# A pooled-attention and mixing kernel on one core: the 1e-9 of the softmax sums as a 73rd column, the pools' 1/8 moved to the copies of x, a subtraction in two pieces, and a new order

## The chip, the core and the metric

The kernel runs on one of the eight cores of a Trainium2 chip. A core has five engines, each with its own queue of instructions that it works off in order: TensorE (PE, with its weight loads shown as PEld), VectorE (DVE), ScalarE (ACT), GpSimd (POOL) and SyncE (SP), which here only issues DMAs. They wait for each other through semaphores. The metric is the device time of one execution in microseconds; the median of three runs is compared.

## The reference, cut to what matters

```python
k_p = k.reshape(B, H, Sp, 8, D).mean(axis=3)        # B, H, S, D = 8, 8, 576, 64; Sp = 72
v_p = v.reshape(B, H, Sp, 8, D).mean(axis=3)
scores = q @ k_p.T / sqrt(D)
attn = exp(scores - scores.max(-1))
attn = attn / (attn.sum(-1) + 1e-09)
x = (attn @ v_p) as [8, 576, 512]
theta = x @ w_theta
y = w_tok_r @ (x * cos(theta)) + w_tok_i @ (x * sin(theta))
u = x + y
out = u + maximum(u @ w_ch, 0)
```

q, k and v come as float32, the four weights as float64, which the kernel turns into float32 itself. The pooled keys and values are kept as sums over 8 rows, not as means, so a factor 1/8 has to be applied to each somewhere: for the keys it is in the scale of the exponential, for the values it is what the change moves.

## The kernel before, in words

All products that need float32 accuracy are made of two rounded parts, a high and a low one (`xh`, `xl` of `x`; `zh`, `zl` of `z`; `uh`, `ul` of `u`; `th`, `tl` and so on of the weights), and three matmuls: high by high, high by low, low by high. The high part is a rounding copy on any engine, the low part a subtraction on DVE or POOL.

The program is a set of generators, one for each step of each batch, and a `yield` ends each piece of a step. A table of words, `SCHEDULE`, names which generator runs its next piece, and a letter behind the word (`a`, `v`, `g`) gives the engine for a piece that can run on several (ACT, DVE, POOL). So the table is the whole order of the program: each engine gets its instructions in the order in which the words stand. Nothing in it is decided while the kernel runs. The words are:

- `k`, `v`, `Q`, `w`, `h`, `c`: loads of keys, values, queries and weights, and their conversion; `K`, `V`: pooling and placing of keys and values; `D`: 24 idle matmul instructions (12 matmuls on an identity tile, line 256)
- `Sb.m` (`soften`): one tile `m` of the attention of batch `b`: scores on PE (lines 661 and 669) into one PSUM tile, maximum (700), subtraction (716), exponential on ACT (720), row sums of 8 heads (722), `sm = (sm + 1e-9) * 8` (729), reciprocal (731), the products `en = e / sm` (734 and 741), and from batch 2 on a transpose of 32x32 blocks into one shared tile `G` (750, 753). Tiles 0 and 1 make the first group of a batch, tiles 2, 3 and 4 the second. In batches 0 and 1 the sums come with the exponentials of ACT, head by head (709), and in batch 0 the 1e-9 and the 8 are put in by ACT (726).
- `Eb.g` (`turn`): 16 DMAs that finish the transpose of a whole group from `G` to `eraw` (816), and its split in two parts (819 to 839). `G` has one buffer, so the next group's write to it has to wait for these DMAs.
- `Xb.g.c` (`attend`): attention times values (863), and a copy of the result from PSUM to `xT` (865; the helper is at lines 175 and 177)
- `Tb.m` (`rotate`): theta (886), cosine and sine, and `z` (913 to 923)
- `Zb.c` (`take`): `zh` and `zl` of 128 of the 512 columns of `z` (935 and 937); `Mb.c.h` (`mix`): the 27 matmuls of the token mix for one such block and one part of the rows (951), the addition to `xT` (957), `uh` and `ul` (962, 964). Part `h=0` has 256 rows and uses `zl` in its last nine matmuls, part `h=1` has 320 rows and uses `zl` in its first nine. Two PSUM buffers serve `py` and the `pf` of the next step.
- `Fb.c.h` (`final`): the last product (980), its addition (986), a transpose (999) and the store (1005).

While one batch is in `M`, the next but one is in `S` and `E`; while it is in `F`, the next one is in `T`.

Of the kernel before, what the change touches and what calls it, by code (L numbers as in the profile page):

```python
# [35 lines left out]
w0.1a S0.3 S0.1v X0.0.0 w2.0 S0.2g S0.2g S0.2 X0.0.0a h1v h1 h3 h3 h3v S0.2a S0.2 S0.4 S0.4 S0.4 h2 w0.1 h3v
w0.1 h3 h3 h3v S0.3g S0.3g S0.3 S0.2a X0.0.1 X0.0.1v h3 h3a X0.0.3 X0.0.3a S0.3a S0.4 w0.1g W0 S0.4g S0.4g k1.1
w1.1 w1.1 w1.1a h2v S0.4 S0.4a S0.4 S0.4a h2 X0.0.2 W0v W0 h3 X0.0.2a T0.0v K1.1g S0.3 S0.3a X0.2.0 w3.1 T0.1v
T0.1g w2.0 w2.0a w2.0v T0.0g X0.2.0a W0 W0v W0 w2.1 w2.1 k1.2 w1.1a w1.1 w1.1 Q1.0 Q1.1 w3.0 Q1.1 Q1.1a Q1.0
Q1.0a X0.2.3 X0.2.3a w2.0 X0.2.1 X0.2.1a w2.1a w2.1a w2.1 w1.1v w2.1 w2.1g T0.0 T0.0 T0.0 v1.0 V1.0g W1 W1v W1  # L40
w3.0 T0.0 T0.0 T0.0a X0.2.2 X0.2.2v T0.2g w3.0a w3.0v K1.2g T0.0 T0.0 Q1.2 Q1.3 Q1.3 Q1.3v T0.1 T0.1 W1 w3.1
w3.1a X0.2.3g T0.0 W1v T0.1 T0.1 T0.1 Q1.2 T0.1a W1 T0.2v T0.2 w2.0 w2.0v w3.0 w3.0 w3.1a w3.1 T0.4a v1.1 T0.2
T0.2 T0.3a T0.3g T0.1 T0.1 T0.1 W2 W2a W2 T0.2 T0.2 c0 T0.2a T0.2 T0.2 T0.2 Q1.2a T0.3 T0.3 w4.0 w4.0 w4.0a
T0.4g T0.4 w3.0g T0.3 T0.3 T0.3 T0.3a w4.0v w4.0 w3.1 V1.1g T0.4 W2 w4.0 W2a W2 T0.4 w3.1v W3 T0.4 T0.4 T0.3
T0.3 T0.3 c0 c0a w4.0g Q1.4 Q1.4 T0.4 T0.4 W3a K1 K1a K1 W3 c0 W4 c0 c0 c0g Z0.0a Z0.0v M0.0.0 c0g c0g W4a W4
W4a W4 W4a W4 W4a W4 c1 M0.0.0 W3 W3a W3 Z0.1v Z0.1v M0.0.1 c1 c1a c1 c1 c1 K1a c1v c1a k2.2 K2.2v c1v c2 Z0.2a
M0.0.0a M0.0.1 M0.0.1a S1.0 S1.0 c2 M0.1.0 M0.1.0 Q1.4v c2v c2 c2 v1.2 V1.2v c2 c2v M0.1.1 M0.1.1 M0.1.1v S1.0
S1.0 S1.0v Z0.3a Z0.3v c2a c2v Z0.2g M0.2.0 M0.2.0 S1.0v V1a V1g V1 c3 M0.1.0v M0.1.0g c3 S1.1 S1.1 S1.1 c3v c3
c3 c3 c3g c3a c3g M0.2.1 M0.1.1g M0.2.1 S1.0 S1.0v S1.0 S1.0 S1.0a M0.3.0 S1.1 S1.1v S1.1v M0.2.0a M0.2.0g S1.0
S1.2 S1.2 S1.2 S1.1 S1.1v S1.1 S1.1 S1.1v S1.1 M0.3.1 V1g M0.3.0 M0.3.0a V1g S1.2 X1.0.0 X1.0.0a M0.3.1 M0.3.1a  # L50
S1.2v S1.2v S1.3 S1.3 S1.3 M0.3.0g X1.0.1 X1.0.1v M0.0.0g M0.0.1v M0.2.1g M0.2.1g M0.3.1v F0.0.0 X1.0.3 F0.0.0
X1.0.3v F0.0.1 F0.0.1 F0.0.0 F0.0.1 X1.0.2 k2.0 S1.2 K2.0g X1.0.2a S1.3 S1.2a S1.2 S1.2 S1.2a S1.4 S1.4 S1.2
Q2.0 Q2.0 S1.3g v2.2 S1.3g F0.1.1 F0.1.1 S1.3 S1.3v S1.3 S1.3 S1.4 S1.4 S1.4v S1.4v T1.0g S1.3a S1.3 T1.0g T1.0
T1.0 T1.0 T1.0 S1.4 S1.4a S1.4 S1.4 S1.4a S1.4 F0.1.0 F0.0.1 X1.2.0 X1.2.0v T1.0 T1.0a T1.0 k2.1 K2.1g K2 K2a
Q2.1 Q2.1 X1.2.3 X1.2.3a T1.1g T1.1g T1.1 T1.0 T1.0 F0.1.0 F0.1.0 X1.2.1 X1.2.1a v2.0 V2.2g V2.0v v2.1 T1.1 T1.1
T1.1 X1.2.2 X1.2.2a T1.3v F0.1.1 F0.1.1 T1.2g T1.2g T1.3g V2.1g V2g k3.2 K2 K2a S2.0 S2.0 T1.1 T1.1a F0.2.0
F0.2.0 T1.1 T1.1 T1.1 S2.0 S2.0 T1.2 T1.2 T1.2 S2.0g S2.0v F0.2.1 T1.2 F0.2.1 F0.2.0 F0.2.1 T1.2 T1.2a X1.2.3a
k3.0 S2.1 S2.1 K3.2g K3.0g T1.2 T1.2 T1.2 S2.0 S2.1 S2.1 S2.1g T1.3 T1.3 S2.1g T1.3 T1.3 S2.1 S2.2 S2.2 T1.4a
T1.4g Q3.0 V2g T1.3 T1.3a T1.3 F0.2.1 V2 V2g V2g T1.3 T1.3 F0.3.0 F0.3.0 F0.3.0 T1.4 T1.4 T1.4 T1.4 T1.4 S2.3
k3.1 S2.2 K3.1v K3 S2.2 S2.2g T1.4 T1.4 S2.2v F0.3.1 F0.3.1 Z1.0a Z1.0v M1.0.0 S2.3 Z1.1a Z1.1g E2.0 S2.2 S2.4  # L60
# [1065 lines left out]
```

## Time and profile before

| what | value |
|---|---|
| median of 3 runs | 633.87 us (633.78 to 636.93) |
| the profiled execution | 635.37 us, of which span 633.6 us |
| PE busy | 602.3 us (95%) |
| DVE busy | 482.1 us (76%) |
| ACT busy | 300.8 us (47%) |
| POOL busy | 354.1 us (56%) |
| instructions | 11412 |
| mean granted TensorE clock | 0.977 |

The share of busy time is an average over stages of different kinds: loads and weight conversion up to about 76 us, the first batch with the rest of the conversion up to about 182 us, then the steady part, then the last product. "Idle before" in a group of instructions is time in which the engine stood still just ahead of them, and the name behind it is what ended the wait. A busy PE is not a PE at its peak, since matmuls are pipelined and their ends are modelled. An engine's idle time costs nothing unless something waits for what it does next.

### The profile page before, as it was taken

To read this page: it belongs to the slowest core of one execution; us is meant where nothing else is said; L and a number is where in the kernel's file an instruction comes from. 1 tells how busy PE (TensorE), PEld (TensorE's weight loads), DVE (VectorE), ACT (ScalarE), POOL (GpSimd) and SP (SyncE) were. 2 spreads that over 40 slices of the span, in tenths; PEclk is the share of its full clock that TensorE was granted. 3 is DMA by queue.
4 is the path that set the end of the run, shared out by engine and by line. 5 is a ranking of instruction groups with operands and counts; after the bars stand their busy time and mean duration, and the time that the engine had idled before them with its cause. 6 is when DMAs were issued, how large, how long until landed. Compare 5 with 4: busy or idle time off the path is not lost.

```text
span 633.6 us, 11412 instructions
## 1 busy us (share of the span) xinstructions
PE 602.3 (95%) x4120; PEld 556.4 (88%) x4120; DVE 482.1 (76%) x893; ACT 300.8 (47%) x655; POOL 354.1 (56%) x382
## 2 busy tenths in 40 slices
PE   7899989799899999999999999899999999999995
PEld 6766879788689989998899989888999999999995
DVE  6587979988878989689876888867977698556233
ACT  5577956567863454237532573036524452144110
POOL 2345631656764667867657677665448545541520
PEclk9599969899999999999999999999999999999999
DMA  9972412345855647473625546235444240511204
GB/s 291 245 229 67 113 43 70 70 84 116 141 95 95 107 93 134 89 125 72 110 53 101 98 87 140 44 56 104 82 69 71 48 66 10 82 19 26 33 2 76
DMA packets 235130, 57.85 MB, mean 91 GB/s; under 512 B 223169, under 2 KB 223681, under 8 KB 235073
## 3 DMA queue, kind: packets, MB, share of 16 engines
q1 hardware_dynamic: 233888, 56.97, 45.6%
q8 instruction: 33, 0.54, 0.4%
q10 hardware_dynamic: 1184, 0.15, 0.2%
q14 instruction: 25, 0.20, 0.1%
HBM read 37.81 MB, written 9.44 MB: 75 GB/s over the span
## 4 chain that ended last, share of the span: by engine, by line
PE 66%; DVE 17%; SPq 6%; ACT 3%; DMA 3%; issue 2%; POOL 0%; DVEq 0%; ACTq 0%; POOLq 0%
PE py L951 24%; PE pf L980 13%; PE pt L886 13%; SPq L816 6%; PE pv L863 6%; PE s L669 3%; PE px L896 2%; DMA eraw<-G 2%; DVE ul L964 1%; DVE mx L700 1%; DMA kpst<-in_k_dram 1%; DVE G L750 1%; PE pq L577 1%; PE s L661 1%; DVE en L734 1%
## 5 line engine op out<-in xcount | busy, mean ns | idle before, releaser
L951 PE MATMUL py<-WTh,zh 128*128 128x256 f32 (+1 forms) x576 | 87.8, 300 | 3.9 <-DVE xT L957 2.7
L951 PE MATMUL py<-WTl,zh 128*128 128x256 f32 (+1 forms) x576 | 88.8, 300 | 0.0
L951 PE MATMUL py<-WTh,zl 128*128 128x256 f32 (+1 forms) x576 | 86.4, 297 | 0.0
L951 PEld LDWEIGHTS py<-WTh,zh 128*128 128x128 f32 x576 | 81.0, 191 | 4.8 <-issue 1.8
L951 PEld LDWEIGHTS py<-WTl,zh 128*128 128x128 f32 x576 | 82.0, 194 | 0.0
L951 PEld LDWEIGHTS py<-WTh,zl 128*128 128x128 f32 x576 | 78.9, 191 | 0.2
L937 POOL TENSOR_TENSOR zl<-z,zh 128x1152 fp32r<-128x1152 f32 x20 | 55.1, 2759 | 31.4 <-ACT zh L175 19.1
L879 POOL TENSOR_TENSOR xl<-xT,xh 128x512 fp32r<-128x512 f32 x33 | 44.6, 1357 | 43.6 <-ACT xh L175 30.8
L957 DVE TENSOR_TENSOR xT<-py,xT 128x256 f32<-128x256 f32 (+1 forms) x64 | 28.1, 442 | 42.9 <-PE py L951 42.9
L964 POOL TENSOR_TENSOR ul<-xT,uh 128x256 fp32r<-128x256 f32 (+1 forms) x40 | 33.8, 857 | 34.0 <-ACT uh L175 18.9
L720 ACT ACTIVATE e<-e 128x576 f32<-128x576 f32 (+1 forms) x30 | 20.6, 686 | 60.0 <-DVE e L716 59.9
L980 PE MATMUL pf<-uh,chh 128*128 128x320 f32 (+1 forms) x256 | 46.7, 305 | 0.0
L980 PE MATMUL pf<-ul,chh 128*128 128x320 f32 (+1 forms) x256 | 45.6, 298 | 0.9 <-DVE ul L964 0.9
L886 PE MATMUL pt<-th,xh 128*128 128x512 f32 x160 | 44.9, 402 | 0.2
L890 ACT ACTIVATE g<-pt,c_magic 128x512 f32<-128x512 f32 x38 | 26.1, 686 | 39.6 <-PE pt L886 32.9
L980 PE MATMUL pf<-uh,chl 128*128 128x320 f32 (+1 forms) x256 | 44.5, 296 | 0.0
L886 PE MATMUL pt<-th,xl 128*128 128x512 f32 x160 | 43.4, 393 | 0.6 <-POOL xl L879 0.6
L886 PE MATMUL pt<-tl,xh 128*128 128x512 f32 x160 | 43.8, 396 | 0.0
L669 PE MATMUL s<-kpT,qT 128*128 128x144 f32 x256 | 40.8, 306 | 2.0 <-DVE ri L731 0.9
L175 ACT COPY xT<-pv 128x320 f32<-128x320 f32 (+1 forms) x43 | 17.1, 398 | 50.2 <-PE pv L863 46.9
L669 PEld LDWEIGHTS s<-kpT,qT 128*128 128x128 f32 x256 | 36.3, 203 | 3.8 <-ACT spare L709 1.2
L980 PEld LDWEIGHTS pf<-ul,chh 128*128 128x128 f32 x256 | 38.0, 189 | 1.7 <-DVE ul L964 1.7
(250 smaller groups left out, 1441.0 us busy)
## 6 DMA issues: line engine op xcount, KB each, us to landing
out_dram<-R SPq DMA_DIRECT2D x112, 72.0 KB, 2.1
kpst<-in_k_dram SPq DMA_DIRECT2D x15, 512.0 KB, 4.1
vpst<-in_v_dram SPq DMA_DIRECT2D x28, 256.0 KB, 3.8
qsst<-in_q_dram SPq DMA_DIRECT2D x96, 72.0 KB, 3.3
eraw<-G SPq DMA_DIRECT2D x96, 60.0 KB, 2.3
eraw<-G SPq DMA_DIRECT2D x96, 40.0 KB, 2.1
WTh_st<-in_moe_w_theta_dram SPq DMA_DIRECT2D x4, 512.0 KB, 8.7
wcraw<-in_moe_w_ch_dram SPq DMA_DIRECT2D x4, 512.0 KB, 3.9
```

The source lines that it names most:

```text
L669: nc.tensor.matmul(scs[c // 2][:n, 2 * SP * (c % 2) : 2 * SP * (c % 2 + 1)], qT[:, c, t0 : t0 + n], kpT[:, c, :], start=True, stop=True,)
L720: nc.scalar.activation(e[:n], e[:n], AF.Exp, scale=scale)
L816: nc.sync.dma_start(blocks(Ex, jj, i), blocks(Gx, i, jj))
L863: nc.tensor.matmul(pv[:, :gn], l, r, start=i == 0, stop=i == len(terms) - 1)
L879: ENG[pick()].tensor_tensor(xl, xT[:, :, o], f32(xh), ALU.subtract)
L886: nc.tensor.matmul(pt, l[:, c, :], r[:, c, :], start=i == 0, stop=i == 11)
L890: nc.scalar.activation(g, pt, AF.Identity, bias=c_magic)
L937: ENG[pick()].tensor_tensor(zl, z[:, :, o], f32(zh), ALU.subtract)
L951: nc.tensor.matmul(py[:, :n], l[:, kk, :], r[:, kk, t], start=i == 0, stop=i == 3 * NK - 1)
L957: nc.vector.tensor_tensor(u, py[:, :n], u, ALU.add)
L964: ENG[pick()].tensor_tensor(ul[:, c, t], u, f32(uh[:, c, t]), ALU.subtract)
L980: nc.tensor.matmul(pv[:, :n], l[:, kk, o], uhl[r][:, kk, t], start=i == 0, stop=i == 11)
```

## The change

Four edits, beside the order. (1) The exponentials go to one constant tile `e_eps` of 8 x 73 columns, of which column 73 holds 1e-9 from a fill at the start; the row sum is taken over all 73, which makes the separate `(sm + 1e-9) * 8` on DVE go. (Tiles 1 and 3 of batch 0 keep their own tile.) In batches 0 and 1, where the sums come from ACT, the 1e-9 is added by an instruction of ACT right behind the exponentials. (2) The 1/8 of the pooled values is applied where `xT` is copied from PSUM: the copy becomes an activation with a scale on ACT, or a multiplication on DVE. (3) `zl` is made by two instructions, of 640 and 512 columns a partition, on the same engine. (4) The zero tile at the start is a part of `G`. The line numbers move by one to three: what was line 722 is 727, 731 is 729, 734 is 732, 750 is 748, 951 to 964 are three higher.

```diff
+    e_eps = const([P, 8, SP + 1], F32, "e_eps")
+    nc.gpsimd.memset(e_eps, 1e-9)
+
+    G = const([P, 5 * 3 * P], F32, "G")
+    nc.gpsimd.memset(G, 0.0)
+    zero = G[:, 0:512]
...
-        e = temp(b, m, "e", 8 * SP).rearrange("p (x g) -> p x g", g=SP)
+        if split:
+            e = temp(b, m, "e", 8 * SP).rearrange("p (x g) -> p x g", g=SP)
+        else:
+            e = e_eps[:, :, 0:SP]
...
                     bias=mx[:n, x : x + 1], scale=scale, accum_out=sm[:n, x : x + 1],
                 )
+            nc.scalar.activation(sm[:n], sm[:n], AF.Identity, bias=c_eps[:n])
             yield
...
             nc.scalar.activation(e[:n], e[:n], AF.Exp, scale=scale)
             yield
-            nc.vector.tensor_reduce(sm[:n], e[:n], AX.X, ALU.add)
-            if b == 0:
-                yield
-        if b == 0:
-            nc.scalar.activation(sm[:n], sm[:n], AF.Identity, bias=c_eps[:n], scale=float(POOL))
-            yield
-        else:
-            nc.vector.tensor_scalar(sm[:n], sm[:n], 1e-9, float(POOL), ALU.add, ALU.mult)
+            nc.vector.tensor_reduce(sm[:n], e_eps[:n], AX.X, ALU.add)
...
-        copy(pick(), xT[:, c, g0 : g0 + gn], pv[:, :gn])
+        if pick() == "a":
+            nc.scalar.activation(xT[:, c, g0 : g0 + gn], pv[:, :gn], AF.Copy, scale=1.0 / POOL)
+        else:
+            nc.vector.tensor_scalar(xT[:, c, g0 : g0 + gn], pv[:, :gn], 1.0 / POOL, None, ALU.mult)
...
-        ENG[pick()].tensor_tensor(zl, z[:, :, o], f32(zh), ALU.subtract)
+        for r in (slice(0, 5), slice(5, NK)):
+            ENG[pick()].tensor_tensor(zl[:, r], z[:, r, o], f32(zh[:, r]), ALU.subtract)
```

The order is a new table from its first word to its last; a line of each, the first one:

```diff
-D k0.2 w0.0 w0.0 w0.0a w0.0v w0.0 h0 h0 h0a k0.0 K0.0 h0a h0 h0 h0v h0 h0v h0 h2 h2 k0.1 K0.1 h2a h2a h1 h2 h2
+k0.0 w0.0 k0.1 K0.0 K0.1 w0.0 w0.0a w0.0g w0.0 h0 h0 h0g h0a h0 h0 h0v h1 k0.2 h1 h1a h1a h1 h1 h1g Q0.0 K0.0a
```

Three places show what the table does. First, the head of PE's queue, up to the first scores `s`. Before:

```order
L256 MATMUL warm<-ident 128x128 x12
L516 MATMUL kpp_136<-kpst_0_134,ident 128x128 x8
L350 MATMUL ths_149<-WTh_st,ident 128x512
L351 MATMUL ths_149<-WTl_st,identr 128x512
L516 MATMUL kpp_136<-early,ident 128x128 x8
L518 MATMUL kpp_136<-kprst_119,ident 64x64 x8
L527 MATMUL pk_187<-ident,kp_182 64x128 x4
L577 MATMUL pq_0_198<-ident,qsst_0_196 128x128 x4
L537 MATMUL pkr_206<-ident,kpr_183 64x64
L669 MATMUL s_0_209<-kpT,qT_195 128x144 x4
```

and in the changed kernel:

```order
L517 MATMUL kpp_111<-kpst_0_106,ident 128x128 x8
L517 MATMUL kpp_111<-early,ident 128x128 x8
L519 MATMUL kpp_111<-kprst_144,ident 64x64 x8
L528 MATMUL pk_169<-ident,kp_155 64x128 x4
L578 MATMUL pq_0_177<-ident,qsst_0_153 128x128 x4
L351 MATMUL ths_183<-WTh_st,ident 128x512
L352 MATMUL ths_183<-WTl_st,identr 128x512
L538 MATMUL pkr_188<-ident,kpr_156 64x64
L670 MATMUL s_0_191<-kpT,qT_152 128x144 x4
L257 MATMUL warm<-ident 128x128 x12
```

The idle matmuls went from the front of PE's queue to behind the first scores. On SP's queue the first block of keys (`kpst`) went with them from fourth to first, and the last block (`kprst`) from first to sixth.

Second, DVE at the last tile of the attention of batch 5 (`sm_4`, `en_4`), which runs during the token mix of batch 4 (`py_1_0`). Before:

```order
L722 TENSOR_REDUCE sm_4_4648<-e_4_4646 64x8
L729 TENSOR_SCALAR sm_4_4648<-sm_4_4648 64x8
L731 RECIPROCAL ri_4_4736<-sm_4_4648 64x8
L734 TENSOR_TENSOR en_4_4738<-e_4_4646,ri_4_4736 64x512
L741 TENSOR_TENSOR en_4_4738<-e_4_4646,ri_4_4736 64x64
L750 STREAM_TRANSPOSE G<-en_4_4738 64x4x128
L753 STREAM_TRANSPOSE G<-en_4_4738 64x64
L554 STREAM_TRANSPOSE qT_4326<-qsst_1_4779 128x1152
L957 TENSOR_TENSOR xT_3776<-py_1_0_4751,xT_3776 128x256
```

and in the changed kernel:

```order
L727 TENSOR_REDUCE sm_4_4690<-e_eps 64x8
L729 RECIPROCAL ri_4_4740<-sm_4_4690 64x8
L732 TENSOR_TENSOR en_4_4742<-e_eps,ri_4_4740 64x512
L739 TENSOR_TENSOR en_4_4742<-e_eps,ri_4_4740 64x64
L748 STREAM_TRANSPOSE G<-en_4_4742 64x4x128
L751 STREAM_TRANSPOSE G<-en_4_4742 64x64
L960 TENSOR_TENSOR xT_3754<-py_1_0_4705,xT_3754 128x256
L177 CAST uh_4733<-xT_3754 128x256
L555 STREAM_TRANSPOSE qT_4221<-qsst_1_4672 128x1152
```

The scalar instruction is gone, and the eviction of `py_1_0` went ahead of the transpose of the queries.

Third, DVE a little later, where the next attention tile (batch 6, tile 0) writes `G` again and the block `py_2_1` is evicted. Before:

```order
L722 TENSOR_REDUCE sm_0_4884<-e_0_4882 128x8
L729 TENSOR_SCALAR sm_0_4884<-sm_0_4884 128x8
L731 RECIPROCAL ri_0_4889<-sm_0_4884 128x8
L734 TENSOR_TENSOR en_0_4891<-e_0_4882,ri_0_4889 128x512
L741 TENSOR_TENSOR en_0_4891<-e_0_4882,ri_0_4889 128x64
L750 STREAM_TRANSPOSE G<-en_0_4891 128x4x128
L753 STREAM_TRANSPOSE G<-en_0_4891 128x64
L177 CAST eh_256_4895<-eraw_256_4894 128x1280
L957 TENSOR_TENSOR xT_3776<-py_2_1_4916,xT_3776 128x320
```

and in the changed kernel:

```order
L727 TENSOR_REDUCE sm_0_4848<-e_eps 128x8
L729 RECIPROCAL ri_0_4852<-sm_0_4848 128x8
L443 TENSOR_TENSOR kprst_4585<-kprst_4585 64x256
L443 TENSOR_TENSOR kprst_4585<-kprst_4585 64x128
L448 TENSOR_TENSOR kpr_4855<-kprst_4585 64x64
L177 CAST eh_256_4891<-eraw_256_4890 128x1280
L1002 STREAM_TRANSPOSE R_3_4910<-oT_3_1_4593 128x320
L960 TENSOR_TENSOR xT_3754<-py_2_1_4862,xT_3754 128x320
L1002 STREAM_TRANSPOSE R_3_4910<-oT_3_0_4564 128x256
L748 STREAM_TRANSPOSE G<-en_0_4914 128x4x128
L751 STREAM_TRANSPOSE G<-en_0_4914 128x64
```

The write to `G` went from ahead of the eviction of `py_2_1` to behind it, and the products `en` of this tile went to POOL.

Over the whole program the table moves 11 of the 40 subtractions `xl` from POOL to DVE (7 there before, 18 now).

More of the change, by code (lines that the diff above doesn't have):

```diff
@@ L36 @@
[L36 to L60, printed above, removed]
@@ new lines @@
+F0.0.0 F0.0.0 F0.0.0 F0.0.1 S1.3 S1.3 X1.0.3 X1.0.3a S1.2 S1.2a S1.2 S1.2 S1.2a S1.4 S1.4 S1.3g S1.3g S1.3
+F0.1.1 S1.2 k2.1 K2.1v Q2.0 T1.0g T1.0v S1.4 S1.4 S1.3a S1.3 S1.3 S1.3a S1.3 F0.0.1 T1.0 T1.0 S1.4g S1.4g S1.4
+T1.0 S1.4a S1.4 S1.4 v2.0 S1.4a S1.4 F0.1.0 F0.1.0 V2.0v T1.0 T1.0 T1.0a T1.1g T1.0 T1.0 T1.0 X1.2.0 X1.2.0a
+F0.1.1 K2 K2v Q2.1 T1.1g T1.1 T1.1 X1.2.3 X1.2.3a T1.1 T1.1 X1.2.2 X1.2.2a T1.1 K2 K2a X1.2.1 T1.1a X1.2.1a
+T1.2a v2.1 V2.1g V2g V2g Q2.1 S2.0 S2.0 k3.2 T1.3a k3.0 T1.2v T1.2 T1.1 T1.1 T1.3g T1.1 S2.0 T1.2 F0.1.0 F0.1.1
@@ new lines @@
+S5.2v S5.2 T4.2 T4.2 T4.4g T4.4g T4.2a T4.2 T4.2 E5.0v E5.0a T4.2 F3.1.1 S5.3 F3.1.0 F3.1.1 F3.1.0 F3.1.1 T4.3
+T4.3 T4.3 T4.3 T4.3 T4.3a T4.3 E5.0g E5.0v T4.3 T4.3 S5.3 F3.2.0 F3.2.0 T4.4 T4.4 T4.4 V5g v6.2 V6.2g F3.2.1
+F3.2.1 v6.0 V6.0g F3.1.1 T4.4 T4.4 T4.4 F3.2.0 F3.2.1 T4.4 S5.4 F3.3.0 F3.3.0 F3.3.1 X5.0.0 k7.2 K6v K6 K6a
+F3.3.1 X5.0.0v Z4.0g Q6.0 Z4.0g M4.0.0 X5.0.1 v6.1 V6.1g M4.0.1 Z4.1v Q6.1 S5.3 S5.3 S5.3v S5.3g S5.4 S5.3
+X5.0.1a M4.0.0 M4.0.1 X5.0.2 X5.0.2v Z4.1g M4.1.0 M4.0.0v M4.0.1a M4.0.0v S5.4 S5.4 S5.4v S5.4v S5.4 k7.0 M4.1.0
@@ new lines @@
+T6.1 T6.1 M5.3.0 X6.2.3 M5.2.1v X6.2.3a M5.3.0 M5.3.0v M5.3.0g T6.1 T6.1 T6.1a T6.1 T6.1 T6.1 T6.2a F5.0.1
+F5.0.1 F5.0.0 F5.0.0 F5.0.0 F5.0.1 v7.1 S7.2 V7.1g S7.2 E7.0 F5.0.1 T6.2g T6.2 T6.2 T6.2 T6.2 X6.2.3a T6.4a
+T6.4v T6.2 T6.2v T6.3g T6.3v T6.2 T6.2 T6.2 F5.1.1 F5.1.1 T6.3 T6.3 V7a V7g V7 V7g E7.0g E7.0v E7.0g T6.3 T6.3
+F5.1.0 F5.1.0 F5.1.0 F5.1.1 F5.2.1 F5.2.1 F5.1.1 T6.3 T6.3a T6.3 T6.3 T6.3 T6.4 T6.4 T6.4 T6.4 T6.4 F5.2.0
+F5.2.0 F5.2.0 F5.2.1 T6.4 T6.4 F5.2.1 F5.3.0 F5.3.0 F5.3.1 F5.3.1 S7.2 S7.2 S7.2v E7.0g S7.2v S7.2 V7g X7.0.0
@@ L131 @@
+Z7.2v Z7.2v M7.2.0 M7.1.1 M7.1.1g M7.2.0 M7.2.0a Z7.3g Z7.3g M7.3.0 M7.3.0 M7.3.0g M7.2.0v M7.3.1 M7.3.1 F6.3.1
+F6.3.0 F6.3.1 M7.3.0v M7.2.1 M7.2.1 M7.1.1v F7.0.0 F7.0.0 F7.0.0 F7.1.0 F7.1.0 M7.3.1g M7.3.1g M7.2.1a M7.2.1g
+F7.0.1 F7.0.1 F7.1.0 F7.0.1 F7.1.1 F7.1.1 F7.1.1 F7.0.1 F7.2.0 F7.2.0 F7.1.1 F7.2.1 F7.2.1 F7.2.1 F7.2.0 F7.2.1
+F7.3.1 F7.3.1 F7.3.1 F7.3.0 F7.3.0 F7.3.0 F7.3.1
 """
@@ L214, in tile_attn_moe @@
     c_eps = const([P, 1], F32, "c_eps")
-    nc.vector.memset(c_eps, 1e-9 * POOL)
+    nc.vector.memset(c_eps, 1e-9)
     c_cos = const([P, 1], F32, "c_cos")
@@ L223, in tile_attn_moe @@
     nc.gpsimd.memset(kpT, 0.0)
-    zero = work([P, 8 * SP], F32, "e", "zero")[:, 0:512]
-    nc.gpsimd.memset(zero, 0.0)
+    e_eps = const([P, 8, SP + 1], F32, "e_eps")
[3 more added lines that the diff above has]
+    zero = G[:, 0:512]
     Vh = const([P, NC, P], F32R, "Vh")
@@ L230, in tile_attn_moe @@
     nc.scalar.copy(Ve.rearrange("p c n -> p (c n)"), zero)
-    G = const([P, 5 * 3 * P], F32, "G")
-    nc.gpsimd.memset(G, 0.0)
     th = const([P, NC, DM], F32R, "th")
```

154 lines of the change are left out of this document (80 added, 74 removed).

## The prediction

> **What bounds the kernel now.** I read the page's busy times and its chain of waits first, then busy times stage by stage, then the single waits.
>
> ```profile
> PE 602.3 (95%) x4120; PEld 556.4 (88%) x4120; DVE 482.1 (76%) x893; ACT 300.8 (47%) x655; POOL 354.1 (56%) x382
> PE 66%; DVE 17%; SPq 6%; ACT 3%; DMA 3%; issue 2%; POOL 0%; DVEq 0%; ACTq 0%; POOLq 0%
> 0.00:16.00 16.00, 11.87 (x77) 10.56 (x77) 10.89 (x21) 8.90 (x14) 4.36 (x11) 1.00 0.92 290
> 16.00:32.00 16.00, 13.40 (x63) 11.82 (x64) 8.15 (x17) 8.86 (x48) 5.61 (x6) 0.57 1.07 243
> 32.00:76.00 44.00, 42.68 (x257) 30.88 (x256) 36.80 (x67) 35.56 (x98) 24.11 (x26) 1.00 0.55 146
> 76.00:182.00 106.00, 94.85 (x640) 86.13 (x639) 90.86 (x174) 74.21 (x198) 57.53 (x64) 0.94 0.42 84
> 182.00:396.00 214.00, 211.65 (x1488) 199.63 (x1487) 178.59 (x324) 95.84 (x169) 150.28 (x167) 1.00 0.55 101
> 396.00:420.00 24.00, 21.28 (x158) 20.78 (x158) 18.40 (x29) 3.82 (x8) 14.63 (x11) 1.00 0.27 42
> 420.00:600.00 180.00, 179.74 (x1248) 169.93 (x1247) 126.48 (x242) 70.48 (x118) 92.90 (x94) 1.00 0.33 57
> 600.00:634.00 34.00, 26.85 (x203) 26.64 (x201) 11.94 (x25) 3.15 (x6) 4.73 (x6) 0.97 0.23 36
> ```
>
> The rows of stages give, after the length, busy time of PE, PEld, DVE, ACT and POOL, then the granted clock, the DMA share and GB/s. PE is the bound wherever it is fed: it misses 2.4 us in 182 to 396 and 0.3 us in 420 to 600. It stands still in four places: 6.7 us in the first 32 us, where the DMA engines are full (0.92, 1.07); 11.2 us in 76 to 182, where DVE has 90.9 us of work in 106; 2.7 us in 396 to 420; and the 7.2 us at the end, mostly the last transposes and stores, which the change leaves as they are. So a gain can come from two places, and everything else can only lose.
>
> **The place at 396 to 420** shows what edit (1) removes.
>
> ```profile
> 395.64 1.56 POOL L964 TENSOR_TENSOR ul<-xT,uh 128x256 fp32r<-128x256 f32 x2
> 397.17 2.72 POOL L937 TENSOR_TENSOR zl<-z,zh 128x1152 fp32r<-128x1152 f32 x1
> 396.45 3.46 DVE L729 TENSOR_SCALAR sm<-sm 64x8 f32<-64x8 f32 x1
> 400.18 0.68 DVE L734 TENSOR_TENSOR en<-e,ri 64x512 f32<-64x512 f32 x1
> 403.45 1.31 PE L951 MATMUL py<-WTh,zh 128*128 128x256 f32 x9 [1.61 <-DVE xT L957]
> 401.89 12.02 SPq L816 DMA_DIRECT2D eraw<-G  x16
> 415.87 0.71 DVE L750 STREAM_TRANSPOSE G<-en 128x512 f32<-128x512 f32 x1 [2.92 <-DMA eraw<-G]
> 417.87 1.33 PE L951 MATMUL py<-WTh,zh 128*128 128x256 f32 x9 [1.12 <-DVE xT L957]
> ```
>
> An instruction on 8 numbers a partition took 3.46 us: it ended at 399.91, with POOL's `zl` (399.89), after sitting through three POOL subtractions. It made DVE late, so PE waited 1.61 us; it delayed the writes to `G`, so the 16 DMAs (12.02 us of issuing) began late, the next write to `G` waited 2.92 us for them, and PE 1.12 us more.
>
> ```profile
> L729 DVE TENSOR_SCALAR sm<-sm x35: 129/172/3457, 109.8 to 535.2; 128x8 f32<-128x8 f32 x28, 64x8 f32<-64x8 f32 x7
> L729 DVE TENSOR_SCALAR sm<-sm 128x8 f32<-128x8 f32 x28 | 9.8, 351 | 0.8
> L729 DVE TENSOR_SCALAR sm<-sm 64x8 f32<-64x8 f32 x7 | 4.4, 632 | 0.2
> ```
>
> All 35 take 9.8 + 4.4 = 14.2 us of DVE, against 35 x 0.172 = 6.0 at the median; 8.2 us are such waiting. At 396 the change can give back between 0 and 2.7 us. In the changed order (third place shown) the write to `G` also stands behind the eviction of `py_2_1` instead of ahead of it, so that even where it waits, PE has two free PSUM buffers. I take **-2.0 us**.
>
> **Stage 76 to 182.** Its waits on the PE side:
>
> ```profile
> PE pe L762 <- DVE en L734: 2.6, 2, 2.3
> PE wt L396 <- DVE WTl L407: 1.6, 1, 1.6
> PE pk L527 <- DVE kp L447: 1.4, 1, 1.4
> PE py L951 <- ACT zh L175: 1.2, 1, 1.2
> L741 DVE TENSOR_TENSOR en<-e,ri 128x64 f32<-128x64 f32 x15 | 5.5, 369 | 0.1
> L177 DVE COPY qT<-pq 128x512 f32<-128x512 f32 x5 | 3.4, 689 | 1.9 <-PE pq L577 1.8
> L937 DVE TENSOR_TENSOR zl<-z,zh 128x1152 fp32r<-128x1152 f32 x12 | 17.3, 1442 | 1.3 <-ACT zh L175 1.2
> L879 DVE TENSOR_TENSOR xl<-xT,xh 128x512 fp32r<-128x512 f32 x7 | 4.8, 685 | 0.9 <-POOL xh L177 0.9
> ```
>
> Columns behind the bar: total us, mean ns, idle before. Three of the four waits (times and longest at the end of a row) are for DVE. I counted, in the old and the new order, what stands on DVE ahead of the first eviction of `py` of batch 1. Gone are 8 scalars at 0.172 (1.4 us), one `zl` at 1.442, two copies `qT` at 0.689 (1.4) and four small products `en` at 0.369 (1.5); new are three `xl` at 0.685 (2.1). That is 3.6 us less. Other copies and conversion steps move both ways, about as many on as off; I take them at 0. DVE fills 90.86 / 106 = 0.86 of the stage, so I let that share through: 3.6 x 0.86 = **-3.1 us**. The bounds are -11.2 (all of PE's idle time goes) and +4 (the new table breaks as often as the old one did in two of its four waits, 2.6 + 1.4).
>
> **The other costs.** (2) The 1/8 in the copies, (3) two pieces, and the 1e-9 on ACT:
>
> ```profile
> L175 ACT COPY qT<-pq 128x512 f32<-128x512 f32 x3 | 1.6, 561 | 0.0
> L354 ACT ACTIVATE th<-ths 128x512 fp32r<-128x512 f32 x1 | 0.6, 597 | 0.3 <-PE ths L351 0.3
> L356 DVE TENSOR_SCALAR th<-ths 128x512 fp32r<-128x512 f32 x3 | 2.0, 664 | 1.0 <-PE ths L351 1.0
> L726 ACT ACTIVATE sm<-sm,c_eps 128x8 f32<-128x8 f32 x4 | 1.2, 296 | 0.1
> L937 POOL TENSOR_TENSOR zl<-z,zh 128x1152 fp32r<-128x1152 f32 x20 | 55.1, 2759 | 31.4 <-ACT zh L175 19.1
> L879 POOL TENSOR_TENSOR xl<-xT,xh 128x512 fp32r<-128x512 f32 x33 | 44.6, 1357 | 43.6 <-ACT xh L175 30.8
> ```
>
> With a scale, ACT's evacuation of PSUM takes 597 ns instead of 561, DVE's 664 instead of 689: 41 x 0.036 = 1.5 us more on ACT, nothing on DVE. Batch 1's five sums cost 5 x 0.296 = 1.5 us on ACT. ACT is busy 47%; its work hides them, and uncovered they would be 3.0 us. For `zl` two POOL sizes give (2759 - 1357) / 640 = 2.19 ns an element and 236 ns fixed, so 20 second instructions cost 4.7 us on POOL (56% busy); DVE's rows give (1442 - 685) / 640 = 1.18 ns and 79 ns, 0.9 us for 12. The first piece is ready after 236 + 640 x 2.19 = 1.64 us instead of 2.76, so matmuls that start on `zl` may start 1.1 us sooner, the last piece 0.24 later. I take 0, bounds -1 and +5. The 73rd column adds 8 elements to a sum over 576 elements, about 10 ns each. The 11 `xl` that go to DVE cost 11 x 0.685 = 7.5 us there over the program, in stages where DVE has 35 us (182 to 396) and 53 us (420 to 600) to spare: 0.
>
> **The start.** K's first block moves from fourth to first in SP's queue, and the idle matmuls behind the scores.
>
> ```profile
> L256 PE MATMUL warm<-ident x24: 420/421/581, 1.4 to 6.4; 128*128 128x128 f32 x24
> L896 PE MATMUL px<-ident,xT x160: 270/273/435, 61.4 to 580.1; 128*128 128x128 f32 x160
> 8.80 2.02 PE L516 MATMUL kpp<-kpst,ident 128*128 128x128 f32 x16 [1.96 <-DMA kpst<-in_k_dram]
> 18.10 2.26 PE L669 MATMUL s<-kpT,qT 128*128 128x144 f32 x8
> 8.00:18.10 10.10, 7.54 (x60) 6.13 (x61) 6.31 (x12) 5.40 (x13) 0.00 (x0) 0.96 1.17 312
> ```
>
> The first idle matmuls took 421 ns each, like the slowest `px` (435, in a stretch of half clock) and not like its median (273): PE starts at half speed whatever the clock column says (1.00), and by 8.80 it is at full speed (2.02 / 16 = 0.126 us each). In the new order that work is what finds PE cold. Keys come earlier, PE is slower: I take 0, since the DMA engines are full in both stretches and the bytes are the same; bounds -4 (the wait of 1.96 us and as much again) and +4 (below).
>
> **Sum.** -2.0 - 3.1 + 0 + 0 = -5.1 on the span of 633.6, 628.5. The profiled execution took 635.37 with 1.8 around its span, so 630.3 for it. The median of the runs shown is 1.5 us lower, 633.87; the same difference on it gives **628.8 us**.
>
> **Rivals.** *The wait is inherited.* The scalar is gone, but `en` behind it has two operands in SBUF, and POOL is still subtracting. If `en` is held as the scalar was, then at 396.45 the reciprocal runs, and `en` waits until 399.89: it started at 400.18 and now starts 0.3 us sooner, and both PE waits stay. For it: POOL's queue is the same; against it: en's neighbours on POOL are new, and the two pieces of `zl` end sooner. Then -2.0 becomes -0.2, and DVE's relief in 76 to 182 is the median's 1.4 us at most: 633.87 - 0.2 - 1.2 = 632.5. The Trainium skill ("SBUF — State Buffer", Who interferes with whom) says that the pair of ports which DVE shares with GpSimd is locked for a whole instruction, by DVE instructions in a two-port mode such as a scalar operation, and by those with two SBUF inputs against a GpSimd instruction that reads SBUF. The scalar's end with POOL's agrees; by that rule it would be this rival.
>
> *A cold start.* PE's work between 8.00 us and the first scores is 7.54 us, nearly all at full speed (the row of that stretch). At half speed that is 7.5 us more. By the shapes in the code 1.2 MB less stand ahead of the first keys (128 KB of `kprst`, 576 of weights, 512 of `WTh`), 3.9 us at the 312 GB/s of the same row, so scores would come 3.6 us later than 18.10, and with them every tile behind. It decides if they start after 18.1. With the new order's gains lost in it, 633.87 + 3.6 = 637.5: slower. The Trainium skill ("TensorE: Matmul & The Clock Gate", What's actually happening) calls the halved clock the default that some 3.4 us of activity release; the 421 ns agree with it, and by that rule alone the start would go this way.
>
> *All of it.* The new order closes the stage of DVE and the place at 396: 633.87 - 11.2 - 2.7 = 620.0. For it: PE has work in that stage; against it: DVE is at 0.86 and loses only 3.6 us.
>
> **Chances.** Forecast 0.47, inherited 0.24, cold start 0.20, all of it 0.09. The range goes from 619.0, the last case less a little, to 638.5, the cold start and a little. A difference of 0.5% (3.2 us) is about what a measurement of this kernel can tell from no change. Faster by more takes the forecast and the last case, 0.56; within 0.5% the inherited wait, 0.24; slower 0.20.
>
> **What would show it.** Right: no DVE instruction of the softmax above 1 us between the row sums and the write to `G`; PE's idle time in 76 to 182 at about 8 us and near 0 in the stretch that answers to 396 to 420; first scores near 18 us. Inherited: `en` on DVE with single times of 2 us and more. Cold: `kpp` at 0.25 us each and scores after 20 us. The prediction is wrong if PE gets a new idle stretch of 3 us or more in what is now 182 to 600, where the order has no reserve that I can read.

## The result: 628.89 us, and the profile after

| | before | changed |
|---|---|---|
| median of 10 runs | 633.83 us | 628.89 us |
| lowest to highest | 633.11 to 636.93 | 625.43 to 632.45 |
| ratio, 95% interval | | 0.9918 (0.9891 to 0.9945) |
| the profiled execution, its span | 635.37, 633.6 us | 629.07, 627.3 us |
| PE busy | 602.3 us | 591.2 us |
| PE idle in the span | 31.3 us | 36.1 us |
| granted clock, mean of the profiled execution | 0.977 | 0.996 |

Two of the twelve executions of the kernel called run 2 below, at 644 us, lie more than 1.5% above its fastest and are left out of its row.

The time is the one that was forecast, 628.8. The two lines on PE say that it did not come about as forecast: in the profiled executions PE waits 4.8 us *more* than before, and is busy 11.1 us *less* with the same 4120 matmuls. Work that takes less time without being less work has run at a higher clock. These are the page's line of busy times of the changed kernel and its strip of granted clock in 40 slices:

```profile
PE 591.2 (94%) x4120; PEld 545.7 (87%) x4120; DVE 481.5 (77%) x878; ACT 312.6 (50%) x674; POOL 350.2 (56%) x380
PEclk9999999999999999999999999999999999999999
```

Its rows of stages at the cuts used for before (length; busy time of PE, PEld, DVE, ACT, POOL; clock, DMA share, GB/s):

```profile
0.00:16.00 16.00, 8.08 (x54) 7.31 (x55) 9.36 (x17) 7.64 (x13) 9.16 (x15) 0.96 0.95 293
16.00:32.00 16.00, 14.41 (x104) 12.36 (x104) 9.70 (x20) 12.40 (x62) 5.87 (x6) 0.93 0.97 258
32.00:76.00 44.00, 41.02 (x243) 29.33 (x243) 41.48 (x70) 35.87 (x85) 26.33 (x27) 1.00 0.49 140
76.00:182.00 106.00, 96.17 (x694) 88.15 (x693) 91.22 (x175) 77.67 (x209) 62.03 (x72) 1.00 0.45 92
182.00:396.00 214.00, 209.65 (x1473) 197.22 (x1472) 178.35 (x322) 100.54 (x173) 131.76 (x145) 1.00 0.52 97
396.00:420.00 24.00, 23.02 (x166) 22.29 (x166) 18.97 (x33) 7.15 (x14) 16.28 (x17) 1.00 0.57 98
420.00:600.00 180.00, 178.34 (x1251) 168.74 (x1250) 121.44 (x223) 70.90 (x120) 96.03 (x97) 1.00 0.29 47
```

The same strip of the kernel before:

```profile
PEclk9599969899999999999999999999999999999999
```

The trace lists the stretches of half clock exactly. Before had three, 17.3 to 31.0, 82.2 to 92.4 and 123.1 to 126.5 us: 27.3 us in all. The changed kernel has one, 3.4 us. At half clock PE loses half of that time: 13.7 us against 1.7. The difference of 12.0 us is close to the 11.1 us by which PE is less busy. It needn't be the same: PE also waits inside these stretches, and the 24 idle matmuls of the start took 5.49 us ahead of the first keys before and take 2.84 us behind the scores now. (These two executions are ones with much and with little half clock; the means over all runs follow below.)

PE's idle time, stage by stage, from the rows (length less busy time): 0 to 32 us from 6.7 to 9.5; 32 to 76 from 1.3 to 3.0; 76 to 182 from 11.2 to 9.8; 182 to 396 from 2.4 to 4.4; 396 to 420 from 2.7 to 1.0; 420 to 600 from 0.3 to 1.7. Two stages gain 3.1 us together, as two did in the forecast (5.1 there), and four lose 7.8. Not all of the 7.8 us is made by the new order: a PE at full clock is through with its work sooner and then waits for the same loads and evictions, as run 3 below shows.

The new waits, from the list of PE's waits of the changed kernel (total us, times, longest):

```profile
PE kpp L517 <- DMA kpst<-in_k_dram: 4.4, 1, 4.4
PE py L954 <- DVE xT L960: 3.8, 2, 2.8
PE kpp L519 <- ACT kp L175: 3.2, 1, 3.2
PE wt L397 <- DVE WTl L435: 2.3, 1, 2.3
```

The first is the head of the queue, where the idle matmuls stood before. The largest in the steady part is the 2.8 us. The timeline of the changed kernel there, POOL, DVE and PE in turn (start, length, engine; in brackets the idle time and what ended it):

```profile
258.54 2.56 POOL L881 TENSOR_TENSOR xl<-xT,xh 128x512 fp32r<-128x512 f32 x2
261.07 2.80 POOL L940 TENSOR_TENSOR zl<-z,zh 128x640 fp32r<-128x640 f32 x2
259.00 5.88 DVE L443 TENSOR_TENSOR kpst<-kpst 128x512 f32<-128x512 f32 x2 [1.74 <-DMA kpst<-in_k_dram]
264.91 0.29 DVE L448 TENSOR_TENSOR kp<-kpst 128x128 f32<-128x128 f32 x1
265.12 0.48 DVE L960 TENSOR_TENSOR xT<-py,xT 128x320 f32<-128x320 f32 x1
265.66 1.34 PE L954 MATMUL py<-WTh,zh 128*128 128x256 f32 x9 [2.77 <-DVE xT L960]
```

The new table put the sums of the first block of keys of batch 5 on DVE. They began at 259.00, as soon as their load had landed, and the first of the two took 5.42 us (the longest of that line). It ended when POOL's four subtractions did, 258.54 to 263.87. This is the picture of the scalar at 396 in the kernel before, in another place and with an ordinary sum.

### The profile page after: what moved, and what is told of

The parts are those of the page before. It is cut to its first block, busy times and chain, and to the rows that moved or that the text cites. A ratio compares the mean times of both kernels' runs of the same rounds, so it can differ in the third digit from the quotient of the medians.

```text
span 627.3 us, 11459 instructions
## 1 busy us (share of the span) xinstructions
PE 591.2 (94%) x4120; PEld 545.7 (87%) x4120; DVE 481.5 (77%) x878; ACT 312.6 (50%) x674; POOL 350.2 (56%) x380
## 4 chain that ended last, share of the span: by engine, by line
PE 59%; DVE 14%; SPq 10%; DMA 7%; ACT 4%; issue 3%; POOL 3%; DVEq 0%; POOLq 0%; ACTq 0%
PE py L954 24%; PE pf L983 12%; PE pt L888 11%; SPq L814 8%; PE pv L861 4%; PE s L670 3%; DMA out_dram<-R 2%; PE px L898 2%; DMA eraw<-G 1%; DMA WTh_st<-in_moe_w_theta_dram 1%; SPq L1008 1%; DVE kpst L443 1%; DVE R L1002 1%; DMA kpst<-in_k_dram 1%; DVE xT L960 1%
## 5 line engine op out<-in xcount | busy, mean ns | idle before, releaser
L940 POOL TENSOR_TENSOR zl<-z,zh 128x640 fp32r<-128x640 f32 (+1 forms) x40 | 59.5, 1509 | 29.4 <-ACT zh L175 28.9
L967 POOL TENSOR_TENSOR ul<-xT,uh 128x320 fp32r<-128x320 f32 (+1 forms) x41 | 34.6, 849 | 43.6 <-DVE uh L177 29.1
L983 PE MATMUL pf<-uh,chh 128*128 128x256 f32 (+1 forms) x256 | 47.1, 305 | 0.3 <-DVE xT L960 0.3
L983 PE MATMUL pf<-ul,chh 128*128 128x256 f32 (+1 forms) x256 | 44.8, 296 | 0.0
L983 PE MATMUL pf<-uh,chl 128*128 128x256 f32 (+1 forms) x256 | 44.5, 296 | 0.0
L894 DVE SCALAR_TENSOR_TENSOR g<-g,pt 128x512 f32<-128x512 f32 x38 | 25.8, 680 | 24.1 <-ACT g L892 23.8
L725 ACT ACTIVATE e_eps<-e_eps 128x576 f32<-128x576 f32 (+1 forms) x30 | 20.6, 686 | 45.4 <-DVE e_eps L721 45.3
L865 ACT ACTIVATE xT<-pv 128x320 f32<-128x320 f32 (+1 forms) x41 | 16.8, 410 | 51.3 <-PE pv L861 45.6
L881 POOL TENSOR_TENSOR xl<-xT,xh 128x512 fp32r<-128x512 f32 x22 | 30.0, 1368 | 20.2 <-ACT xh L175 16.6
L989 DVE SCALAR_TENSOR_TENSOR oT<-pf,xT 128x256 f32<-128x256 f32 (+1 forms) x64 | 28.5, 449 | 14.2 <-PE pf L983 13.5
```

Source lines behind the costliest of these rows:

```text
L881: ENG[pick()].tensor_tensor(xl, xT[:, :, o], f32(xh), ALU.subtract)
L894: nc.vector.scalar_tensor_tensor(g, g, MAGIC, pt, ALU.subtract, ALU.subtract)
L940: ENG[pick()].tensor_tensor(zl[:, r], z[:, r, o], f32(zh[:, r]), ALU.subtract)
L967: ENG[pick()].tensor_tensor(ul[:, c, t], u, f32(uh[:, c, t]), ALU.subtract)
L983: nc.tensor.matmul(pv[:, :n], l[:, kk, o], uhl[r][:, kk, t], start=i == 0, stop=i == 11)
L989: nc.vector.scalar_tensor_tensor(oT, pv[:, :n], 0.0, xT[:, c, t], ALU.max, ALU.add)
```

## The experiments

Every run's median stands beside that of the kernel before on the same chip (634.2 to 634.6 in the three sets). "Lost" is the mean over a kernel's runs of (1 - granted clock) x span. It is 11.8 us in 61 runs of the kernel before, and 4.4 us in the 10 of the changed one.

| kernel | median us | ratio (95%) | lost us |
|---|---|---|---|
| changed kernel | 628.9 | 0.9918 (0.9891 to 0.9945) | 4.4 |
| 1: new code, table of before | 628.8 | 0.9925 (0.9890 to 0.9960) | 9.6 |
| 2: old code, new table | 638.9 | 1.0070 (1.0038 to 1.0102) | 7.1 |
| 3: before, 23 idle matmuls | 630.1 | 0.9935 (0.9910 to 0.9960) | 4.2 |
| 4: changed, 21 idle matmuls | 627.3 | 0.9887 (0.9850 to 0.9924) | 3.0 |
| 5: as 1, `zl` in one piece | 627.6 | 0.9883 (0.9838 to 0.9927) | 9.3 |
| 6: as 1, scalar back | 635.0 | 1.0008 (0.9984 to 1.0031) | 11.0 |
| 7: changed, scalar back | 634.1 | 0.9995 (0.9966 to 1.0024) | 5.0 |
| 8: as 1, 23 idle matmuls | 627.0 | 0.9888 (0.9854 to 0.9921) | 5.7 |
| 9: changed, one sum to POOL | 625.8 | 0.9859 (0.9831 to 0.9886) | 3.3 |
| 10: changed, `zl` in one piece | 629.6 | 0.9924 (0.9896 to 0.9951) | 3.5 |
| 11: changed, 4, 9 and 10 together | 625.6 | 0.9862 (0.9838 to 0.9886) | 1.7 |
| 12: table of before, 5 and 8 together | 624.7 | 0.9848 (0.9824 to 0.9873) | 5.3 |

Two theories stood against each other. W (waits), that of the prediction: the time came from shorter waits of PE. C (clock): it came from PE running at full clock.

### 1 and 2: code and table apart

Run 1 has the new code and the table of before; of each batch-0 tile's words one is gone, since its step is gone. A place of it:

```diff
-Q0.1v S0.1 S0.0 S0.0 S0.0 S0.1 S0.1 Q0.3 Q0.3
+Q0.1v S0.1 S0.0 S0.0 S0.1 S0.1 Q0.3 Q0.3
```

> The changed kernel's code (edits 1 to 4) with the table of before (less one word for each tile of batch 0, whose step is gone). Theory W (waits, as predicted): the place at 396 gives back 2.0 us and DVE's relief by the scalars 1.2 us, so 633.8 - 3.2 = 630.6, at the clock of before (0.977). Theory C (clock: the gain is that PE runs 24 us less at half clock, which only the new order brings): the half clock stays at about 27 us in the first 130 us, and the time at 632.5 to 634.

Run 2 has the old code and the new table, with that word put in:

```diff
-h2g S0.0 S0.0 S0.0 Q0.2 Q0.2
+h2g S0.0 S0.0 S0.0 S0.0 Q0.2 Q0.2
```

> The code of before with the new table (one word more for each tile of batch 0). Theory W: the scalar and its 3 us wait on POOL are back, only the new order's share of DVE's relief is left: about 632. Theory C: half clock under 10 us, mean clock 0.985 to 0.997, and a time between 627 and 632 that moves with the clock.

Run 1 took 628.8 us, as little as the whole change; run 2 took 638.9, 4.6 us more than the kernel before. So neither theory was right as it stood. All of the net gain is in the code, and the table adds nothing to it. But it does two things that cancel: under the new code it takes the loss at half clock from 9.6 to 4.4 us, and PE's idle time in the profiled executions goes up from 30.0 us (596.3 busy in 626.3) to 36.1.

How much a microsecond of lost clock costs can be read from the runs of one kernel among themselves, since the same program gets different clocks. In the changed kernel's ten runs the span goes up by 0.89 us for each us lost (correlation 0.90; 625.43 us of device time at a clock of 0.997, 632.45 at 0.986). In the runs of before it is 0.53 (correlation 0.80): a part of its half clock lies in the start, where PE waits for other things. So the table's 5.2 us of clock are worth some 3 to 5 us, and what it adds in waits costs about as much. That the two cancel is worked out and not tried: no run has the table's clock without its waits.

### 3, 4 and 8: the clock without the waits

```diff
+    def fill(i, n, tag):
+        p = bank([P, 512], tag, f"fill{i}")
+        for _ in range(n):
+            nc.tensor.matmul(p[:, 0:P], ident, ident, start=True, stop=True)
+        yield
...
-K0.2 K0.0a K0.2v K0.1a K0 K0a
+K0.2 K0.0a K0.2v K0.1a Y0 K0 K0a
-W2a W2 T0.4 w3.1v W3 T0.4
+W2a W2 T0.4 w3.1v Y1 W3 T0.4
-S1.2 S1.2 S1.2 S1.1 S1.1v
+S1.2 S1.2 S1.2 Y2 S1.1 S1.1v
```

Nothing reads what these matmuls write. They only give PE something to do where it waits, 8, 6 and 9 of them in runs 3 and 8; in run 4 there are two places, with 12 and 9.

> The kernel before, with 23 idle matmuls added on PE where it waits: 8 ahead of the transposes of the first keys (about 15 us), 6 ahead of the fourth block of token weights (79 us), 9 ahead of the transposes of the second tile of batch 1 (119 us). No wait is made shorter. Theory W: nothing gained, 633.5 to 636. Theory C: at most two windows of half clock are left (under 7 us instead of 27), each us of half clock gone saves 0.4 us: 624 to 628, faster than the changed kernel.

> The changed kernel with 21 idle matmuls: 12 in the wait at 10 to 13 us, 9 in the wait at 88.5 to 90.8 us. Theory W: 629, as without them. Theory C: mean clock 0.995 or more in every run, 625 to 627, and a spread of the runs of under 3 us instead of 7.

> The new code with the table of before and the 23 idle matmuls in the three waits. Theory C (half clock and waits add up): the loss at half clock falls from 9.6 to 4 us as it did in the kernel before (12.3 to 4.2, 4.2 us faster), so 625 to 626.5, below the changed kernel. If the new code had already removed the stretches that the fill removes: 628 to 630, the fill's own time of about 1 us on top.

Run 3 is the clean test. It makes no wait shorter and adds work, and it is 4.2 us *faster* than before (630.1 against 634.3), with 4.2 us lost instead of 11.8. Theory W had 633.5 to 636. The size is smaller than I expected (624 to 628): 7.6 us less lost, at the 0.53 us a microsecond read above, are 4.0. No run puts the same idle matmuls where PE does not wait. Run 4 gained 1.6 us (627.3; the expectation had at most 627), its runs lying 5.5 us apart and not under 3, with a clock down to 0.991. Run 8 gained 1.8 us on run 1, half a microsecond less than the least that was expected. These two gains point the same way, but the intervals of the ratios overlap (runs 4 and changed, 8 and 1), so run 3 alone shows it clear of noise.

Its busy line and clock strip show what run 3 did: 46 more matmul instructions than before, and 3.4 us less of busy time. The 46 are busy for 5.8 us; with 29.2 us of idle time that makes 35.0 us in which PE does nothing for the result, against 31.3 before. So in the profiled executions 10.2 us less are lost at half clock (14.6 and 4.4), the span falls by 5.5 us (633.6 to 628.1), and most of the rest comes back as time in which PE has no work.

```profile
PE 598.9 (95%) x4166; PEld 553.5 (88%) x4166; DVE 486.3 (77%) x893; ACT 300.7 (48%) x655; POOL 354.7 (56%) x382
PEclk8989999999999999999999999999999999999999
```

### 5 and 10: `zl` in one piece

```diff
-        for r in (slice(0, 5), slice(5, NK)):
-            ENG[pick()].tensor_tensor(zl[:, r], z[:, r, o], f32(zh[:, r]), ALU.subtract)
+        ENG[pick()].tensor_tensor(zl, z[:, :, o], f32(zh), ALU.subtract)
```

> The new code with the table of before (628.8, first set), but zl in one instruction again. If the shorter scalar chain (edits 1 and 2) carries the gain of the code, it stays at 628 to 630; if the two pieces carry it (the last nine matmuls of a block start 1.1 us sooner), the time goes to 632 to 634. Both at a mean clock of 0.980 to 0.990.

> The changed kernel with zl in one instruction. By the pair with the table of before (628.8 with two pieces, 627.6 with one) the second piece gains nothing, and 627 to 629 comes out here too; by the idea that the first piece lets PE start sooner, it is slower, 630 to 632.

627.6 against 628.8 with the old table, 629.6 against 628.9 with the new one: opposite signs, both within the intervals. Run 5 is 0.4 us below its 628 to 630, and run 10 lies between its two ranges. Edit (3) moves nothing that these runs can tell.

### 6 and 7: the scalar put back

```diff
-            nc.scalar.activation(sm[:n], sm[:n], AF.Identity, bias=c_eps[:n])
+            if b == 0:
+                nc.scalar.activation(sm[:n], sm[:n], AF.Identity, bias=c_eps[:n])
...
-            nc.vector.tensor_reduce(sm[:n], e_eps[:n], AX.X, ALU.add)
+            nc.vector.tensor_reduce(sm[:n], e[:n], AX.X, ALU.add)
+        if b > 0:
+            nc.vector.tensor_scalar(sm[:n], sm[:n], 1e-9, 1.0, ALU.add, ALU.mult)
```

> The new code with the table of before, but with the scalar instruction (sm + 1e-9) back on DVE in batches 1 to 7, the row sum over 576 again; xT scale and zl in two pieces stay. If edit 1 carries the gain: 632 to 634, one scalar of 3 us or more behind a row sum; if the two pieces do: 628 to 630.

> The changed kernel (new order) with the same scalar back. The old code in the new order took 639.0 against 628.9: if the scalar is what the new order can't bear, 636 to 639 and the wait of PE for xT grows; if it is the pieces of zl, 628 to 631.

With the scalar back the time is that of before, with either table: 635.0 (ratio 1.0008) and 634.1 (0.9995); run 6 is 1 us above its range. So the 35 small instructions are worth 6.2 us with the old table and 5.2 with the new one. The loss of clock is nearly the same with it and without (11.0 against 9.6 us, 5.0 against 4.4), so little of that is clock. Run 7 came out below the 636 to 639 that I expected. Run 2 is 4.8 us above run 7, so the old code has something beside the scalar that suits the new table badly; no run takes it apart.

Where the scalar costs its time is not where I had looked. These are the same place in run 1 (DVE, POOL) and in run 6 (DVE), the fifth attention tile of batch 5:

```profile
390.87 4.22 DVE L732 TENSOR_TENSOR en<-e_eps,ri 64x512 f32<-64x512 f32 x1
397.17 0.38 DVE L960 TENSOR_TENSOR xT<-py,xT 128x256 f32<-128x256 f32 x1
390.16 1.56 POOL L967 TENSOR_TENSOR ul<-xT,uh 128x256 fp32r<-128x256 f32 x2
391.69 2.86 POOL L940 TENSOR_TENSOR zl<-z,zh 128x640 fp32r<-128x640 f32 x2
```

```profile
390.99 0.49 DVE L963 TENSOR_TENSOR xT<-py,xT 128x320 f32<-128x320 f32 x1 [1.66 <-PE py L957]
393.62 3.91 DVE L730 TENSOR_SCALAR sm<-sm 64x8 f32<-64x8 f32 x1
400.55 0.38 DVE L963 TENSOR_TENSOR xT<-py,xT 128x256 f32<-128x256 f32 x1
```

Without the scalar, the product `en` behind it takes its place and its wait: 4.22 us, until POOL's run ends. Run 6 enters the place 3.0 us later than run 1 (the eviction at 390.99 stands at 388.01 there) and leaves it 3.4 us later (400.55 against 397.17), so the scalar is worth 0.4 us here, not 2.0. The rest grows elsewhere. I compare the same evictions of `py` and `pf` in both traces. From 92 to 146 us run 6 falls from 2.8 us ahead to 1.3 behind, with two stretches of half clock (119.8 and 140.3 us) where run 1 has none. From there on it grows in small steps: run 6 is behind by 1.4 us at 180, 2.0 at 236, 2.9 at 299, 3.5 at 385 and 4.3 at 424 (4.4 at the end), in a stretch where neither has half clock. So 3.0 of the 4.4 us in these two traces have nothing to do with the clock. The rows of stages give PE 0.6 us of idle time in 182 to 396 in run 1, and 1.9 in run 6, which is 1.3 of the 2.1 us that run 6 falls back there:

```profile
182.00:396.00 214.00, 213.42 (x1506) 201.61 (x1504) 177.30 (x317) 94.52 (x164) 152.52 (x174) 1.00 0.54 99
```

```profile
182.00:396.00 214.00, 212.11 (x1497) 200.40 (x1496) 180.78 (x329) 94.30 (x164) 150.89 (x174) 1.00 0.55 99
```

I had read the 2.4 us that PE misses there before as "fed".

### 9: the one new wait

```diff
-T3.0a T3.0g T3.1a k5.0 K5.0v T3.1g
+T3.0a T3.0g T3.1a k5.0 K5.0g T3.1g
```

> The changed kernel with one letter of its table changed: the sums of the first block of keys of batch 5 run on POOL, not on DVE. In the changed kernel the first of them took 5.42 us on DVE at 259 us, while POOL ran four subtractions (258.5 to 263.9), and PE waited 2.8 us for the eviction behind it. If DVE is held by POOL's run there, as the scalar was at 396, that wait goes and the time falls by 2 to 4 us, to 625 to 627. If the wait is only moved (POOL's zl and xl come 2.7 us later): 628 to 630.

625.8 us, 3.1 less than the changed kernel, in the middle of what was expected. POOL takes 2.11 us for the two sums, and PE's matmuls have no wait there any more. From the timeline of run 9, POOL, DVE and PE:

```profile
259.09 2.11 POOL L443 TENSOR_TENSOR kpst<-kpst 128x512 f32<-128x512 f32 x2
258.33 2.24 DVE L177 CAST uh<-xT 128x320 fp32r<-128x320 f32 x1
262.45 1.33 PE L954 MATMUL py<-WTh,zh 128*128 128x256 f32 x9
```

In the changed kernel these matmuls began at 265.66. The eviction of `py` ahead of the place is 0.7 us earlier in run 9 (at 255), those behind it 3.2 (from 317 on), and the end 3.3. So POOL, with its four subtractions to do as well, took the two sums in 2.1 us where DVE took 5.9. DVE is held here too: the cast of `uh` takes 2.24 us, 0.33 in the changed kernel, until just behind the end of the first sum on POOL. But PE waits for nothing that stands behind it.

### 11 and 12: put together

> The changed kernel with zl in one piece, the keys of batch 5 on POOL and 21 idle matmuls in the waits at 10 and 88 us. If waits and half clock add up: 628.9 - 2 to 4 (keys) - 1.6 (idle matmuls, as in the fourth run) - 0 to 1 (one piece) = 622.5 to 625.5. If one of them eats the others: 626 to 628.

> The table of before, the new sums and the xT scale, zl in one piece and 23 idle matmuls in three waits. From 627.6 (one piece, table of before) less the 1.8 to 4.2 us that the idle matmuls gave twice: 623.5 to 626. If the half clock that they avoid cost nothing here: 628.

Run 11 took 625.6 us, as run 9 alone (625.8): the idle matmuls and the one piece add nothing to it, just above the expected 622.5 to 625.5, though it has the least half clock of all. Run 12 took 624.7, in its range. It has the lowest median (the intervals of runs 9, 11 and 12 overlap), 9.5 us under the kernel before on the same chip (ratio 0.9848) and 4.2 under the changed one, with the *old* table, edits (1) and (2), and 23 idle matmuls.

## Why the prediction was right in number and not in its reasons

The forecast of 628.8 for 628.89 was two errors of opposite sign, the half clock that went (12.0 us lost less in the profiled executions, 7.4 in the means of all runs) and 7.8 us of new waits, neither of which I had counted, around terms that were partly right. That they met at 628.8 is luck. The two errors hang together: in run 3, with the old code and the old order, 10.2 us less lost brought 3.7 us more in which PE has no work. By that share (an estimate) some 4 us of the new waits come with the full clock. The 3.4 us in 182 to 396 and 420 to 600, where neither kernel has half clock, are the new order's own.

- **The place at 396 to 420, -2.0.** PE's idle time in the stretch went from 2.7 to 1.0 us, -1.7, near the forecast. But that the scalar was gone was not enough: with the old table the inherited wait came true (`en` 4.22 us). In the changed kernel `en` is 0.68 us and the small product behind it 1.61; the new order had changed what POOL runs beside them. What I wrote against that rival ("en's neighbours on POOL are new") fits these rows. Of the signs that I had set, the one for the forecast (no such instruction above 1 us) was not met (1.61), and the one for the inherited wait (`en` at 2 us and more) was not reached: the longest `en` on DVE took 1.62 us. I had also misread the lines of before: the scalar sat through two of POOL's subtractions, not three, since the first `ul` ended at 396.37, before the scalar began.

```profile
390.66 0.68 DVE L732 TENSOR_TENSOR en<-e_eps,ri 64x512 f32<-64x512 f32 x1
391.27 1.61 DVE L739 TENSOR_TENSOR en<-e_eps,ri 64x64 f32<-64x64 f32 x1
390.73 3.34 POOL L940 TENSOR_TENSOR zl<-z,zh 128x640 fp32r<-128x640 f32 x2 [2.87 <-ACT zh L175]
```

- **Stage 76 to 182, -3.1.** This is the step that failed. I had counted DVE's work ahead of the first eviction of `py` of batch 1, which came at 181.8 us and now comes at 175.5. The instructions that begin on DVE ahead of it take 160.4 us in all, instead of 160.7. Those that I counted do take 3.6 us less. But the copies and conversion steps that I took at 0 take 3.4 us more, 2.3 of it in two instances of one conversion (`wpow<-wsrc_a`, 1.5 and 1.7 us instead of 0.45). PE's idle time from 76 us to that eviction fell by 1.8 us all the same (11.2 to 9.4), and in the fixed stage by 1.4, less than half of the term. DVE's work as a whole is the same, so a lighter DVE is not what shortened the waits; what did stays open. From the first eviction of batch 0 (93.4 and 92.0 us) to that of batch 1 the program is 4.9 us shorter: PE waits 3.7 us less and is busy 1.3 us less, and before, the half clock at 123.1 to 126.5 lost 1.7 us in it.
- **"A gain can come from two places, and everything else can only lose."** The sentence left out a third place, which stood in the rows that I quoted: the clock of 0.57 in 16 to 32 and of 0.94 in 76 to 182. I used the clock column only to price the start.
- **The start, 0.** First scores came at 18.63 instead of 18.10 us, and PE waited 2.8 us more in 32 us: near 0, in the bounds. The cold start did happen, but it was short. The first 16 `kpp` took 3.70 us, half speed, and the next 16 took 2.05:

```profile
4.35 3.70 PE L517 MATMUL kpp<-kpst,ident 128*128 128x128 f32 x16 [4.35 <-DMA kpst<-in_k_dram]
8.13 2.05 PE L517 MATMUL kpp<-early,ident 128*128 128x128 f32 x16
13.34 1.14 PE L519 MATMUL kpp<-kprst,ident 64*64 64x64 f32 x16 [3.16 <-ACT kp L175]
18.63 1.25 PE L670 MATMUL s<-kpT,qT 128*128 128x144 f32 x8
```

  The rival had priced all of the 7.5 us of work ahead of the scores at half speed. These 16 were, 2.0 us of it, and then the stretch from 14.7 to 18.1 us, which followed PE's wait at 13; the new order's keys, at 4.35 instead of 8.80 us, made up for both.
- **The other costs, 0.** `zl` in two pieces: -0.7 and +1.2 us, nothing clear. The 1/8 and the sums on ACT weren't tried by themselves; run 6, which has all of the new code except that the scalar is back, stands at 1.0008 of before, so edits (2) and (3) and the constant tile cost nothing together that the runs can tell.
- **The stretches "where the order has no reserve that I can read".** There the losses were: +2.0 us in 182 to 396 and +1.4 in 420 to 600, with one wait of 2.77 us, under the 3 us that I had set as the sign.
- **The scalar as a whole.** I had priced it at -2.0 and a share of -1.2 at most by its waits. Taken out alone it is worth 5 to 6 us in the medians. Of the 4.4 us in the two traces 3.0 are small delays in stages where PE seemed fed.

## What to carry to other kernels

Read the granted clock beside the idle time: a wait of PE costs its length and then, in some executions, half of one or more stretches of 3.4 us behind it, so a wait of 2 us can cost about 3 (an estimate: 1.7 us lost in one stretch, at 0.53 to 0.89 us each), and idle matmuls that fill such a wait can pay even though they shorten nothing. When DVE has a very long instance of a short instruction, look at what POOL runs beside it: taking that instruction away hands the wait to the next one, and what took it off PE's path here was another order (`en` at 0.68 us) or moving the work to POOL (run 9). And a forecast that meets the time is not yet a reason: compare busy time and idle time with it.
